# Another order for all engines' work in a block-sparse attention and spectral mixing kernel

## The chip, the core and the metric

The kernel runs on one core of a Trainium2 chip. The core has five instruction queues that matter here: TensorE (PE, matrix products and transposes; its weight loads are listed as PEld), VectorE (DVE), ScalarE (ACT), GpSimd (POOL) and SyncE (SP), which here does nothing but issue transfers. Each engine works through its own list in the order in which it was written and waits on semaphores for what the others have to finish. The metric is the device time of one execution in microseconds (us); less is better.

## The reference

Attention over 4 batches, 8 heads, 768 positions and 64 channels, then a mixing layer on its output (factors of the inputs left out):

```python
# attention: 16-wide local window, plus one summary key and value for each block of 32
k_sum = k.reshape(B, H, nb, 32, D).max(axis=3);  v_sum = v.reshape(B, H, nb, 32, D).mean(axis=3)
scores = concat(mask(scale * q @ k.T), scale * q @ k_sum.T + log(32))
a = softmax(scores);  x = a @ concat(v, v_sum)          # x: (4, 768, 512)
# mixing layer
theta = x @ w_theta
zr, zi = x * cos(theta), x * sin(theta)
u = x + einsum('ts,bsd->btd', w_tok_r, zr) + einsum('ts,bsd->btd', w_tok_i, zi)
out = u + relu(u @ w_ch)
```

All of it is float32. The kernel keeps that precision in the mixing layer by splitting each operand into a rounded high part and the remainder as low part, and adding three products (high by high, high by low, low by high). The weights arrive as 8-byte numbers and are turned into float32 on the chip.

## The kernel before

The function `attn_moe` first writes the whole program down as 2087 operations, each with the engines that may run it, what it reads and what it writes. Then `Program.issue` walks through a table, `ORDER`, which names the operations one after the other, each with the engine that gets it (P, A, V, G, S for PE, ACT, DVE, POOL, SP). That table alone sets the order on every engine and, where an operation may run on two engines, which of them it is. Buffers of a pool are handed out in the order in which they are first touched, so the table also sets who waits for which buffer.

The work, by the names used below. A batch has 6 tiles of 128 positions.

- **Weights** (`load_f64`): a raw block is loaded, then six or seven elementwise steps follow: magnitude (ACT or DVE), clip (DVE or POOL), a shift and two combining steps on DVE, the rounding to the high part (ACT or DVE, line 1342), the low part (DVE or POOL, line 1348). `wth0` to `wth3` hold w_theta, 12 blocks `wt` hold the two token matrices. At the end w_ch is loaded over `wth0` to `wth3`.
- **Attention tile** (`att_tile`, `att_half`, line 1476 onwards): scores `s` on PE, masked minimum on DVE (line 1489), exponential on ACT (line 1493), transpose `p` on PE, copy `pt`, product `av` on PE (line 1502), normalisation to `xn` (lines 1506 to 1515).
- **Turn and theta** (`turn_tile`, `theta_tile`): transpose of `xn` (line 1524), its high and low part `xh` and `xl`, 12 products with `wth` (line 1548), then a chain over ACT, POOL and DVE that reduces the angle and takes sine and cosine (lines 1556 to 1571), the products `w` and `zb` with `xn` (line 1579) and their high and low parts `zh`, `zl`.
- **Mixing** (`mix_step`, line 1600): for each batch two halves of the channels, for each half 6 tiles, for each tile 4 parts of 6 products (a part is one operation on PE). The sums stand in three banks `m`; the third is shared by the two channel groups. When a half is done, four additions on DVE (line 1616) take the sums out, and the result goes to `u_scratch` in memory.
- **Pool swap** (`swap_pools`): when all attention and theta work is done, its buffers are given up and those of the last stage take their place. No buffer of the last stage can be written before that.
- **Output units** (`out_unit`): 8 units; `u` is read back as four pieces `cu`, split into `cuh` and `cul`, multiplied with w_ch (line 1647, 16 operations of 3 products per unit), and added on DVE (line 1652).

PE interleaves all of these: attention and theta of one batch between the mixing parts of the batch before. The second half of the mixing of the last batch is left for after the pool swap and is interleaved with the first output units.

## Time and profile before

| | us |
|---|---|
| median of 3 runs | 501.67 |
| the runs | 500.26 to 502.81 |
| the profiled execution | 498.08 |
| its span, first to last instruction | 496.3 |
| PE busy | 453.7 |
| DVE, ACT, POOL busy | 319.1, 271.6, 102.6 |

A row of a group reads: line, engine, operation, output and inputs, size and count, then busy time, the mean of one in ns, and the idle time ahead of it with what ended it. In a timeline the first number is the start, the second the length, and square brackets hold the idle time before the instruction and what released it. SPq is SP issuing a transfer.

### The profile page before, as it was taken

What the parts mean: (1) busy time and instruction counts of PE and PEld (TensorE: products, weight loads), DVE (VectorE), ACT (ScalarE), POOL (GpSimd) and SP (SyncE); (2) the same over time, 40 slices, a digit from 0 to 9 for tenths busy, and PEclk for the clock granted to TensorE, in tenths of its full rate; (3) what the DMA queues carried; (4) which work ended last, traced back from release to release, by engine and by line L of the source; (5) the groups of instructions that cost most, each with busy time, mean ns of one, the idle gap of its engine ahead of it and who ended that gap; (6) DMA issues with size and microseconds to landing.
All of it is one profiled execution on the core that took longest, in us unless ns stands there. A gap on an engine that the chain in (4) does not pass through costs nothing.

```text
span 496.3 us, 10030 instructions
## 1 busy us (share of the span) xinstructions
PE 453.7 (91%) x3864; PEld 383.0 (77%) x3864; DVE 319.1 (64%) x909; ACT 271.6 (55%) x563; POOL 102.6 (21%) x124
## 2 busy tenths in 40 slices
PE   0876989999999999899979999999999499999997
PEld 0355767688887888788868888888878389999996
DVE  5999899977476687656764746435664494333454
ACT  2498999966455785746666775748753220101100
POOL 2033534324020120113011111220101430321021
PEclk9987999999999999999999999999999879999999
DMA  8999450444314640220413202210202600454653
GB/s 319 383 375 325 153 158 17 128 169 142 84 40 157 206 144 29 70 65 30 160 44 98 87 0 86 65 34 2 55 1 87 230 22 35 135 172 157 213 191 138
DMA packets 30767, 62.12 MB, mean 125 GB/s; under 512 B 3584, under 2 KB 14080, under 8 KB 30720
## 3 DMA queue, kind: packets, MB, share of 16 engines
q1 hardware_dynamic: 30720, 61.49, 37.2%
q8 instruction: 30, 0.49, 0.4%
q14 instruction: 17, 0.14, 0.1%
HBM read 48.90 MB, written 12.58 MB: 124 GB/s over the span
## 4 chain that ended last, share of the span: by engine, by line
PE 65%; DVE 13%; ACT 12%; DMA 4%; issue 3%; POOL 1%; SPq 1%; ACTq 0%; DVEq 0%
PE m L1600 29%; PE c L1647 14%; PE t L1548 10%; PE av L1502 4%; PE p L1496 3%; PE s L1476 3%; DVE e L1489 2%; ACT e L1493 2%; DMA vt<-cst 2%; PE av L1417 2%; DVE f L1391 1%; PE t L1524 1%; DMA q<-qg 1%; DMA cu<-u_scratch 1%; DVE xl L1529 1%
## 5 line engine op out<-in xcount | busy, mean ns | idle before, releaser
L1600 PE MATMUL m<-wt,zh 128*128 128x512 f32 (+1 forms) x768 | 171.9, 345 | 2.2 <-DVE x L1616 2.0
L1600 PEld LDWEIGHTS m<-wt,zh 128*128 128x128 f32 x768 | 119.8, 190 | 19.1 <-DVE x L1616 3.1
L1600 PE MATMUL m<-wt,zl 128*128 128x512 f32 (+1 forms) x384 | 99.1, 339 | 0.5 <-POOL zl L1348 0.4
L1493 ACT ACTIVATE e<-e,st 128x118 f32<-128x118 f32 x192 | 66.4, 388 | 28.0 <-DVE st L1489 27.8
L1647 PE MATMUL c<-cuh,wth 128*128 128x384 f32 x256 | 67.1, 343 | 7.0 <-DVE wth L1342 6.6
L1548 PE MATMUL t<-wth,xh 128*128 128x512 f32 x192 | 64.0, 416 | 5.9 <-ACT x L1342 2.8
L1600 PEld LDWEIGHTS m<-wt,zl 128*128 128x128 f32 x384 | 58.9, 189 | 9.9 <-POOL zl L1348 0.7
L1647 PEld LDWEIGHTS c<-cuh,wth 128*128 128x128 f32 x256 | 46.6, 191 | 8.2 <-issue 6.9
L1342 ACT CAST cuh<-cu 128x384 fp32r<-128x384 f32 x18 | 8.8, 510 | 78.3 <-DMA cu<-u_scratch 78.2
L1489 DVE CUSTOM_DVE_ANT_0 e<-s,cs 128x118 f32<-128x118 f32 x192 | 46.7, 272 | 7.0 <-PE p L1496 4.9
L1548 PEld LDWEIGHTS t<-wth,xh 128*128 128x128 f32 x192 | 35.0, 197 | 15.2 <-issue 5.0
L1647 PE MATMUL c<-cul,wth 128*128 128x384 f32 x128 | 43.9, 343 | 0.0
L1502 PEld LDWEIGHTS av<-v,pt 118*64 118x64 f32 x768 | 27.2, 138 | 15.4 <-issue 6.1
L1548 PE MATMUL t<-wth,xl 128*128 128x512 f32 x96 | 38.8, 404 | 0.0
L1652 DVE SCALAR_TENSOR_TENSOR cu<-c,cu 128x384 f32<-128x384 f32 x32 | 17.1, 553 | 30.9 <-PE c L1647 18.8
L1502 PE MATMUL av<-v,pt 118*64 118x65 f32 x768 | 33.5, 229 | 3.7 <-DVE xn L1515 1.6
L1348 POOL TENSOR_TENSOR cul<-cu,cuh 128x384 fp32r<-128x384 f32 x17 | 19.0, 1130 | 74.0 <-DVE cuh L1342 35.1
L1556 ACT ACTIVATE w<-t,bmagic 128x512 f32<-128x512 f32 x24 | 16.5, 686 | 30.5 <-PE t L1548 23.4
L1496 PE MATMUL p<-cs,e 128*118 128x128 f32 x192 | 30.6, 281 | 2.1 <-ACT pt L1342 2.1
L1348 POOL TENSOR_TENSOR zl<-w,zh 128x512 fp32r<-128x512 f32 x10 | 12.9, 1286 | 78.9 <-ACT zh L1342 60.9
L1558 POOL TENSOR_SCALAR w<-w 128x512 f32<-128x512 f32 x15 | 9.5, 632 | 87.9 <-ACT w L1556 87.8
L1348 POOL TENSOR_TENSOR zl<-zb,zh 128x512 fp32r<-128x512 f32 x15 | 20.1, 1345 | 36.2 <-DVE zh L1342 24.4
(85 smaller groups left out, 712.9 us busy)
## 6 DMA issues: line engine op xcount, KB each, us to landing
v<-vg SPq DMA_DIRECT2D x48, 195.0 KB, 2.8
q<-qg SPq DMA_DIRECT2D x24, 256.0 KB, 4.1
cu<-u_scratch SPq DMA_DIRECT2D x32, 192.0 KB, 3.3
out<-cu SPq DMA_DIRECT2D x32, 192.0 KB, 2.0
kn<-kT SPq DMA_DIRECT2D x6, 798.0 KB, 5.1
wt<-wtr SPq DMA_DIRECT2D x6, 768.0 KB, 9.1
wt<-wti SPq DMA_DIRECT2D x6, 768.0 KB, 10.2
f<-vT SPq DMA_DIRECT2D x12, 384.0 KB, 3.4
```

The costliest lines, as they stand in the source:

```text
L1348: op(f"VG tt {n}", lambda e: V[e].tensor_tensor(dst(), src(), hi().bitcast(F32), op=ALU.subtract), reads, writes)
L1417: product = lambda t, st: lambda: nc.tensor.matmul(pv.get()[:NB].rearrange("n p d -> n (p d)"), member(t), st(), start=(t == 0), stop=(t = ...
L1476: mm("s" if len(parts) == 1 else "s0", [lambda p=p, g=g, h=h, c=c, kk=kk: nc.tensor.matmul(sc[h].get()[ROW[g], p, c], q.get()[ROW[h], p, R ...
L1489: op("V ttr", lambda eng, n=n: nc.vector.tensor_tensor_reduce(e.get()[:, n], sc[n % 2].get()[:, 2 * a + n // 2], mask(m), -SCALE, 3.0e38, ...
L1493: op("A exp", lambda eng, n=n: nc.scalar.activation(e.get()[:, n], e.get()[:, n], AF.Exp, bias=st.get()[:, n:n + 1], scale=-1.0), [(st, n) ...
L1496: mm("tr", [lambda n=n: nc.tensor.transpose(tp.get()[:NK, n], e.get()[:, n], ident()) for n in range(NH)], [e, (cs, "ident")], [tp])
L1502: mm("av", [lambda n=n, g=g: nc.tensor.matmul(xa.get()[ROW[g], n], t.get()[:, n, ROW[g]], v[g].get()[:NK, NH * a + n], start=True, stop=Tr ...
L1548: calls = [lambda t=t, xx=xx, k=k, c=c: nc.tensor.matmul(th.get(), xx.get()[:, c], w_th[c].get()[:, k], start=(c == 0 and t == 0), stop=(c ...
L1556: op(f"A psumb {DM}", lambda e: nc.scalar.activation(r(), th.get(), AF.Identity, bias=bmagic.get(), scale=1.0 / TWO_PI), [th, bmagic], [R])
L1600: nc.tensor.matmul(acc[th], zz.get()[:, r, cc], w_t[s, r].get()[:, k, TT[th]], start=(s == r == t == 0 and (th == 0 or c == 0)), stop=(s = ...
L1647: calls = [lambda t=t, k=k, uu=uu, c=c, co=co, acc=acc: nc.tensor.matmul(acc.get(), w_ch[c].get()[:, k, co * P:(co + 1) * P], uu.get()[:, ...
L1652: op(f"V ttp {HT}", lambda e, co=co, acc=acc: nc.vector.scalar_tensor_tensor(u.get()[:, co], acc.get(), 0.0, u.get()[:, co], ALU.max, ALU. ...
```

## The change

The table `ORDER` is replaced. The operations, their sizes, the buffers and the pools stay as they are, and the numbers of operations on PE and POOL stay at 566 and 120; ACT has 471 in place of 467, DVE 713 in place of 717. All line numbers below the table fall by 29 (line 1342 becomes 1313, line 1616 becomes 1587). The table is a list of steps from one operation's number to the next; it has 1190 rows, now 1161, of which this is the head:

```diff
 ORDER = """
-V+4
-S+60
-V+1,+1,+1,+1
-S+12
...
+S+64
+A+1
+G+1
+V+1,-62,+63,+1,-66
...
```

Three places, as each engine's list reads before and now.

The first is DVE's list at the pool swap, which comes right after the last `zb`: `f` and `wth` belong to the conversion of w_ch, `cuh` and `cul` to an output unit, `x<-m` are the additions that empty the banks of the mixing. Before:

```order
L1579 TENSOR_TENSOR zb<-xn,w 128x512
L1386 TENSOR_SCALAR f<-f 128x512
L1342 CAST cuh<-cu 128x384
L1384 TENSOR_SCALAR f<-wth_4581 128x512
L1387 TENSOR_SCALAR f<-f 128x512
L1389 SCALAR_TENSOR_TENSOR f<-wth_4550,f 128x512
L1391 SCALAR_TENSOR_TENSOR f<-wth_4550,f 128x512
L1342 CAST wth_4622<-f 128x512
L1348 TENSOR_TENSOR cul<-cu,cuh 128x384
L1348 TENSOR_TENSOR wth_4622<-f,wth_4622 128x512
L1616 TENSOR_TENSOR x<-m_4251,x 128x256
```

Now:

```order
L1550 TENSOR_TENSOR zb<-xn,w 128x512
L1355 TENSOR_SCALAR f<-wth_4610 128x512
L1358 TENSOR_SCALAR f<-f 128x512
L1360 SCALAR_TENSOR_TENSOR f<-wth_4610,f 128x512
L1362 SCALAR_TENSOR_TENSOR f<-wth_4610,f 128x512
L1319 TENSOR_TENSOR wth_4622<-f,wth_4622 128x512
L1587 TENSOR_TENSOR x<-m_4323,x 128x512
L1587 TENSOR_TENSOR x<-m_4324,x 128x256 x2
L1587 TENSOR_TENSOR x<-m_4331,x 128x512
```

The rounding of a `cu` piece (second output unit) and the start of another block no longer stand inside the conversion of the first w_ch block; that conversion is now one run. Its magnitude moved from ACT to DVE, its clip from DVE to POOL, its rounding from DVE to ACT. On PE 14 mixing parts of the last batch now lie between its last theta product and the first output product; before there were 13.

The second is DVE's list where the first half of the mixing of the second batch ends (`x<-m`), among the work of later attention tiles. Before:

```order
L1579 TENSOR_TENSOR zb<-xn,w 128x512
L1489 ISA e,st<-s_2518,cs 128x118
L1489 ISA st 128x1
L1348 TENSOR_TENSOR zl<-zb,zh 128x512
L1616 TENSOR_TENSOR x<-m_2024,x 128x256
L1616 TENSOR_TENSOR x<-m_2031,x 128x512
L1489 ISA e,st<-s_2518,cs 128x118
L1489 ISA st 128x1
L1508 RECIPROCAL st<-st 128x4
L1616 TENSOR_TENSOR x<-m_2024,x 128x256
```

Now:

```order
L1313 COPY pt<-p 118x512
L1587 TENSOR_TENSOR x<-m_2025,x 128x512
L1587 TENSOR_TENSOR x<-m_2026,x 128x256
L1587 TENSOR_TENSOR x<-m_2033,x 128x512
L1587 TENSOR_TENSOR x<-m_2026,x 128x256
L1479 RECIPROCAL st<-st 128x4
```

The first of the four additions (`m_2023`) stood five rows above this piece. The four now stand together, behind the last mixing part of that half in the table; before, the first two came ahead of that part in the table, with other work between them.

The third is SP's list of loads near the start; `x<-vn` are the three loads for the block means of v, `cs` 128x128 is the identity that the transposes need. Before:

```order
L1339 DMA wth_113<-wth 128x1024
L1339 DMA cs<-cst 128x354
L1339 DMA x<-vn 128x2x512
L1339 DMA vt<-cst 128x44
L1339 DMA wt_124<-wtr 128x1536
L1339 DMA x<-vn 128x2x512
L1339 DMA q<-qg 128x512
L1339 DMA x<-vn 128x2x512
L1339 DMA v<-vg 96x520
```

Now:

```order
L1310 DMA wth_125<-wth 128x1024
L1310 DMA x<-vn 128x2x512 x2
L1310 DMA wt_181<-wtr 128x1536
L1310 DMA x<-vn 128x2x512
L1310 DMA q<-qg 128x512
L1310 DMA v<-vg 96x520
L1310 DMA cs<-cst 128x128
L1310 DMA v<-vg 96x520
```

The three loads stand a little earlier in the list, and the identity, which was the third load of all, is now the eighteenth.

More of the change, by code (lines that the diff above doesn't have):

```diff
@@ new lines @@
+A-253,+221,+1
+S+25,+1
+V-107,+111
+A-42,+47,-37
+G-219
+A+141
+P+155
+V-295,-6,+7
+P+177
+A+1,-184,+258,+1
+S+115
+A-228
+V+229
+P-149
+S-216,+379,+56
+V-178,-82
+G-184,+395,-1
+V-384
+P+292,-1,+3
+V-298
+P+207
+V-67
+P+157
+V-35
+A-83
+V-38
+A+79
+V+41
+A-53,+42,-108,+122
+V-1,-54
+P-29
+V+30
+A+177
+P-206
+A-180
+P+181
+G-177
+V+1
+A+260
+P-83,+71
+V-111
+P+78,+171
+A-170,+45,-83,+262,-1
+V-438,-5
+A+10
+P+287
+G-286
+V+210,-215
+A+257
+P+35
+A-45,-246
+V+176,+39,-38
+A+1
+P+38
+V-211,+1
+P+241,+12
@@ new lines @@
+V-42
+S+262
+V-43,-1,+2
+A+4,-223
+P+69,-27
+A+1
+V+1,+126
+P-102,+2,+101
+A+96
+P-84
+S-469,+6
+A+281
+V+1,+2
+A+41,+220,-93
+V+1,-170
+A+171
+V+56,+3
+P-162
+V+20,-86
+A+179
+V+48
+P-159,-27,+1,+1,+1,+26
+V+141
+A+5,+15
+V-5
+A+6
+P-52
+A+50
+S-28,-489,+596
+P-46
+A-48,+2
+P+2,-152
+A-22
+G+160,-159
+V+1,+40
+A+142
+V+37
+A-85
+V+1,+1,+82
+A+48
+V-93
+A-172,+222,-221
+G+263
+P-243,+3,+112,+37
+A+1
+V-172
+A+135
+P+48
+V+31,+15,-228
+A+1
+V+1
+P+18
+V+210,-95
+A+129
+P-242
+V+19
+P-17,+2,-3
+A+209,+31
@@ new lines @@
+V-91
+A+1
+V+10
+P+1
+V+32,+13
+A-12
+V-81,+91
+P+38
+A-32,-15,+2
+P+1
+V+47
+P-243
+V+197,-195,+2
+A+156,+130
+P-178
+V-106,+2
+P+105
+S+173,-281
+A+201
+S+29
+A-26
+P-95,+1
+A+1
+G+1
+V+44
+A+1,+129
+V-173
+P+92
+V+45
+P-243,+1
+V+4,+224,-219
+P-7,+148,-149,+4
+G+5
+P-3,+4
+V+4,+229,-228,+229
+S+216
+V+1
+A-230,-126,+1
+V+1
+S+218
+V-95
+A+17,+28
+V-255,+88
+P-103,+2
+S+447,-234
+V+8
+S-61
+P-156
+G+267
+P-266
+V+230,+213
+G-434
+V+88
+S+59,-173
+V+155,+1
+P+33
+V+1,+1,+1
+A+46,+1,+14
+P+31
+A-47,-35
@@ new lines @@
+P+2
+V-129,+1
+P+106
+G-195
+P+112,+7
+S+138
+V+7
+S+45
+A+5,-269
+G+1
+V+1,+1,+219
+S-501,+433
+P-109
+A+140,-12,+10,-32,+33,+39
+P-37
+V+50,-15
+A-173
+V-2,+189
+S-562
+P+396,+7
+S+80
+V-1
+G+2
+P+17
+V-127
+P+2
+V+138,+47
+P-163,-21,+1,+1,+21
+V+160
+P-158,+2
+A+148,+1,-15,-207
+V+1,+2,-1,+2
+A+231
+G+29
+P-190,+1,+2,-1
+A-27
+S-334
+A+519,-63
+G+92,-213
+V+1
+A+1
+V+164
+A+4
+P+3
+A+43
+V-94,+1
+A-120
+V+156,-155,+1,+1,+1
+P+127
+V+1,+1,+1
+P+80
+V-177
+A+143
+V+37
+S-64,+160
+A-270,+140,-12
@@ new lines @@
+A+34,-45,+1
+V-124,+79,+54
+A+4
+P-47
+V+1
+A+35
+P+1
+G-125
+A+47
+V+1,+85
+A+4
+V-88,+41
+A+36,+10
+P-230,-5,+2,+4,+1
+V+183,-41
+A+1,+87
+P-46,+35
+A+1
+V-33
+P+74
+A+52
+P-82
+V+34
+A-33
+V+30,+2,-79,+1,+90,+1
+A+35
+V-34
+A+32
+P-309,+3
+A+262,+2
+V+11,-16
+A+4
+P-79,+1,+1
+A+79
+P-78,-186
+V+216
+G+90
+A-30,-273
+G+1
+V+135,+1,+77,-76
+G+1
+P+86
+V+1
+S+73
+P+7,-44
+V-35
+A+47,-2
+S-24
+V+59
+P-309
+A+186
+G+1
+V+1
+A+77
+V-35
+P-226,-3,+5
+A+183,+88
+V-269
+A+182
+V-180
+S+293,-54
+P+17,-35
@@ new lines @@
+A+1
+P-28,+12,+6,-12,+1,-6
+V-6
+G+1
+V-191
+P+203,+1
+V+16
+A+6
+V-5
+S+7,-269,+40
+G+228,-3
+P-10
+V-9
+P+10,+1
+A+13
+P-32
+V+20
+S+1,-263
+P+253,-10
+S-197
+V+198
+P+10
+S-3
+P+4
+V+1
+S+1,-12
+G+30
+P+19,+1,+1,+1
+V+1
+S+1,+1
+P-24,+1,+1,+10,+1,+1
+S+19
+P-27,-3
+V+1
+S+26,-3
+V-2,+1
+S-21,-231
+P+233,+1,+1,+6
+V+1
+A+12
+V-18
+A+24
+P+8
+A-11
+S-14
+V+12
+S-18,+49
+P-24
+S+27
+A+1
+P-10,-6,-11,+6
+G-11,+3
+P+14,+1
+S+16,+3
+P-14,-11,+1
+V+1,+15
+P-5
+V+6
+P-5,-19,+1
+V+26,-25
+P+11
+V+7,-6
@@ L1236 @@
 P+3,+1
-V+1
-S+1
-P-16,+1,+1
 V+1
```

1914 lines of the change are left out of this document (770 added, 1144 removed).

## The prediction

> **What bounds the kernel now.** I read the page first: which engine is full, where it is not, and whether its clock holds.
>
> ```profile
> span 496.3 us, 10030 instructions
> ...
> PE   0876989999999999899979999999999499999997
> ...
> PEclk9987999999999999999999999999999879999999
> ...
> PE 65%; DVE 13%; ACT 12%; DMA 4%; issue 3%; POOL 1%; SPq 1%; ACTq 0%; DVEq 0%
> ```
>
> PE is full from about 100 us to the end but for one slice, the 32nd (384 to 397 us), and its clock dips there too. A change of order cannot shorten PE's own work; it can only take away PE's waits. So the next view is the waits of PE, longest in total first.
>
> ```profile
> PE s L1476 <- DVE ks L1411: 12.2, 3, 10.4
> PE c L1647 <- DVE wth L1342: 6.6, 1, 6.6
> PE t L1548 <- ACT x L1342: 2.8, 2, 1.6
> PE t L1548 <- DVE xl L1529: 2.3, 3, 1.5
> ...
> PE m L1600 <- DVE x L1616: 2.0, 3, 1.4
> ...
> PE av L1502 <- DMA v<-vg: 0.2, 1, 0.2
> ```
>
> The first is the start, when nothing is loaded yet. The second is one wait at the pool swap. PE's timeline shows it, and the chain of waits from there shows who caused it.
>
> ```profile
> 389.47 0.51 PE L1600 MATMUL m<-wt,zl 128*128 128x512 f32 x2
> 396.62 0.66 PE L1647 MATMUL c<-cuh,wth 128*128 128x384 f32 x1 [6.63 <-DVE wth L1342]
> 397.60 0.69 PE L1647 MATMUL c<-cuh,wth 128*128 128x384 f32 x1 [0.32 <-DVE wth L1348]
> ```
>
> ```profile
> 375.43 0.70 ACT w L1556
> ...
> 380.66 0.69 DVE zb L1579
> ...
> 385.64 5.67 DMA cu<-u_scratch
> ...
> 397.60 2.93 PE c L1647 x8
> 400.53 3.63 PE m L1600 x13
> ```
>
> The wait is not for the weights. In DVE's timeline the conversion of the first w_ch block began at 382.07, then DVE stood until 391.33 at a `cuh` rounding whose piece was still on its way, with the rest of the conversion behind it in the list:
>
> ```profile
> 382.07 0.43 DVE L1386 TENSOR_SCALAR f<-f 128x512 f32<-128x512 f32 x1 [0.73 <-ACT f L1382]
> 391.33 0.65 DVE L1342 CAST cuh<-cu 128x384 fp32r<-128x384 f32 x1 [8.84 <-DMA cu<-u_scratch]
> 391.90 0.41 DVE L1384 TENSOR_SCALAR f<-wth 128x512 int32<-128x512 int32 x1
> 392.69 0.98 DVE L1389 SCALAR_TENSOR_TENSOR f<-wth,f 128x512 int32<-128x512 int32 x1
> 393.70 1.37 DVE L1391 SCALAR_TENSOR_TENSOR f<-wth,f 128x512 uint32<-128x512 uint32 x1
> 396.86 0.68 DVE L1348 TENSOR_TENSOR wth<-f,wth 128x512 fp32r<-128x512 f32 x1
> ```
>
> **The change, part by part.** Sums are made against the profiled execution, span 496.3 and time 498.08; the runs shown have their median at 501.67, 3.6 us above it. I carry the difference in span over to the median.
>
> *The wait at the swap: 6.63 + 0.32 = 6.95 us.* The new order takes the `cuh` rounding out of the conversion. Does something else arrive late in its place? After the last theta product (375.4, where ACT's `w` starts) the angle chain runs to the end of `zb` at 380.66 + 0.69 = 381.35, so the buffers of the last stage come free 5.9 us after it; the new chain has the same steps, on other engines in part, and I leave it at 5.9. In that time and after it PE has mixing parts. A part is 6 products, and 48 products take 8.46 us in this stretch of the chain:
>
> ```profile
> 118.58 8.46 PE m L1600 x48
> ...
> 468.08 24.91 PE c L1647 x141
> ```
>
> So a part takes 1.06 us, and the 14 parts that now lie there 14.8 us. From the free buffers to the end of the parts there are 8.9 us. The conversion in that time, at this stretch's own slow prices: magnitude 0.41 (DVE), clip 0.72 (POOL), shift 0.41, combining 0.98 and 1.37 (DVE), rounding 0.61 (ACT), low part 0.68 (DVE): 5.2 us, and some 0.3 for six handovers. The `cu` piece runs beside it:
>
> ```profile
> 383.80 0.51 ACT L1342 CAST cuh<-cu 128x384 fp32r<-128x384 f32 x1 [1.76 <-DMA cu<-u_scratch]
> 392.41 0.72 POOL L1386 TENSOR_SCALAR f<-f 128x512 f32<-128x512 f32 x1 [0.64 <-DVE f L1384]
> 393.09 1.42 POOL L1348 TENSOR_TENSOR cul<-cu,cuh 128x384 fp32r<-128x384 f32 x1
> 394.48 1.70 POOL L1348 TENSOR_TENSOR zl<-zb,zh 128x512 fp32r<-128x512 f32 x1
> ```
>
> The first piece was there 2.5 us after the buffers came free; with rounding and low part that is 2.5 + 0.51 + 1.42 = 4.4. Both ways are ready 3 to 4 us before PE asks. I take the whole 6.95. Bounds: 0 kept of it at best; at worst a piece that takes the 5.67 of the chain and queues behind POOL's 1.70 is ready after 0.4 + 5.7 + 0.5 + 1.7 + 1.4 = 9.7, and 0.8 us stay.
>
> The combining step that took 1.37 at 393.70, beside a busy POOL, takes half as long where POOL stands:
>
> ```profile
> 19.82 0.69 DVE L1391 SCALAR_TENSOR_TENSOR f<-wth,f 128x512 uint32<-128x512 uint32 x1
> ```
>
> [...]
>
> *The clock after the wait: 2.9 us.* The windows behind it show TensorE at half clock:
>
> ```profile
> 393.00:395.00 2.00, 0.00 (x0) 0.00 (x0) 1.97 (x2) 0.22 (x1) 2.00 (x3) 0.50 0.06 22
> ...
> 401.00:403.00 2.00, 2.00 (x8) 1.71 (x8) 1.97 (x3) 0.00 (x0) 1.49 (x2) 0.50 0.00 0
> 403.00:406.00 3.00, 3.00 (x18) 2.60 (x18) 2.31 (x5) 0.62 (x1) 0.00 (x0) 0.96 0.02 5
> ```
>
> At 24.91 / 141 = 0.177 each, 8 output products take 1.41 us; they took 2.93. 13 mixing products at 0.176 take 2.29; they took 3.63. Together 2.86 us that go with the idle time. Bounds: 0, if a shorter wait still drops the clock, and 2.9. I take 2.9, since no wait is left. [...]
>
> *What the additions cost at the swap.* DVE now goes from the conversion straight to the four additions, which wait for the last mixing parts; the other w_ch blocks queue behind them. PE's list has 4 output operations (3 products, 0.53 us each) and 8 parts before it asks for the second w_ch block: 10.6 us. DVE has in that time the four additions (0.69, 0.42, 0.42, 0.69 in the rows further down) and eleven steps of 0.41 to 0.69, about 6.4 us: 8.6. No wait; I book 0.4 us of loss, bounds 0 and, with the eleven doubled as at 393.70, 4.4.
>
> *The end of a mixing half: 1 us.* In the second batch PE stood in the middle of a part:
>
> ```profile
> 208.52 0.74 PE L1600 MATMUL m<-wt,zh 128*128 128x256 f32 x3 [1.44 <-DVE x L1616]
> ```
>
> ```profile
> 205.64 0.69 DVE L1616 TENSOR_TENSOR x<-m,x 128x512 f32<-128x512 f32 x1
> 208.05 0.42 DVE L1616 TENSOR_TENSOR x<-m,x 128x256 f32<-128x256 f32 x1
> ```
>
> The product shares its bank with the sum that DVE was reading, and the reading was late behind `zb` and `zl`. With all four additions behind the last part this wait goes. The old order has such a crossing, an addition ahead of a last part, at three ends, and all waits of this kind are the 2.0 us of the list above; the new order has it at three other ends (first batch twice, third batch), with PE work of 0.6, 2.8 and 1.4 us between for an addition of 0.42 to 0.69. I take 1 us; bounds -3 and +2.
>
> *The middle otherwise: 1 us.* Two kinds of wait stand in the list above, theta for `x` and `xl`, 2.8 and 2.3. Counting PE work between a tile's turn and its first theta product for tiles 7 to 24: under 3 us at four tiles before, at one now. Between its last `av` and its turn: 2.2 us or less at nine tiles before, at one now. Steps on other engines are in part further back in exchange. Bounds -5 and +4.
>
> *The start: 1 us.*
>
> ```profile
> 10.00:20.00 10.00, 6.69 (x69) 2.84 (x70) 8.84 (x27) 3.63 (x7) 3.15 (x4) 1.00 1.04 395
> 90.00:100.00 10.00, 9.20 (x88) 6.81 (x87) 9.86 (x28) 9.16 (x19) 3.19 (x4) 1.00 0.41 127
> ```
>
> Loads run at 395 GB/s. Up to the third `x<-vn` 6723 KB were asked for, now 6403: 0.8 us earlier, and the identity 515 KB or 1.3 us after it, before the block means are done. From there to 100 us DVE and ACT are nine tenths full, with the same work. I take 1 us; bounds -4 and +4.
>
> Sum: 6.95 + 2.86 - 0.4 + 1 + 1 + 1 = 12.4 us, span 483.9, median **489.3 us**.
>
> **The rivals.** *The wait moves into the first output units* (second and third w_ch block late behind the additions). For: DVE's list there is long. Against: 2 us of cover. Doubled steps give a wait of 15.0 - 10.6 = 4.4, and with the clock's 2.9 the time is 501.7 - 12.4 + 7.3 = 496.6. *No change*: the swap gains its 9.4 and start and middle lose their lower bounds of 4 and 5; about 501. For: PE's middle has small waits at hundreds of places, and all of them are new. *Slower*: the `v` loads.
>
> ```profile
> v<-vg SPq DMA_DIRECT2D x48, 195.0 KB, 2.8
> ```
>
> They land in 2.8 us. SP's list is in order, with the waiting writes of `u_scratch` between them; PE work between the event that frees a `v` load and the product that needs it was 9.3 us or more from the second batch on, and is now 4.8 to 6.7 at four tiles. It decides once a late write in front holds them more than 2 us over that. At six ends of halves with 3.5 us each it costs 21, and the time is 501.7 - 12.4 + 21 = 510. Against: PE waited for `v` 0.2 us in all before.
>
> **Numbers.** The forecast 0.75, the moved wait 0.11, no change 0.07, slower 0.07. About 0.5% (2.5 us) is what a measurement of this kernel can tell from no change. The forecast's own range is 483 to 495; to leave out no more than 2 in 10 I go from 482 to 498. Faster 0.86 (both of the first), same 0.07, slower 0.07.
>
> **What would show it.** Right: no wait of PE over 2 us after 300 us, granted clock 1.00 through the swap, DVE's conversion of the first w_ch block in one piece of 4 to 6 us, PE's last product 10 to 14 us earlier. Wrong: PE `c` waiting for `wth` or `cuh`; `av` waiting for `v`; PE less busy than 9.2 us between 90 and 100 us.

## The result, and the profile after

The changed kernel takes 478.69 us (median of 4 runs, 478.44 to 480.48) beside 502.24 us of the kernel before (4 runs, 500.26 to 503.40): the ratio is 0.954, 95% interval 0.950 to 0.958. A second comparison with more runs gave 481.09 beside 500.36 us, ratio 0.959 (0.956 to 0.962). The forecast was 489.3 us with a range from 482 to 498: the direction is right, the gain, 23.6 and 19.3 us, was 1.9 and 1.6 times what was forecast, and the time lies below the range in both. The comparisons leave out a few slow executions: three of the kernel before at some 506 us, and four of others at 569 to 1502 us (in the one of 1104 us, profiled for swap_three, mixing products came 0.44 us apart in the mean, in place of 0.18 at full clock and 0.30 at half clock in middle_new, and its profile reads a clock of 1.00, so the half clock named in the expectation of swap_three_b is not shown).

The page of the changed kernel, the same rows as before:

```profile
span 476.6 us, 10041 instructions
...
PE   0875979999999999999999999999999999999997
...
PEclk9988899999999999999999999999999999999999
...
PE 78%; DVE 8%; DMA 6%; issue 3%; ACT 2%; POOL 1%; SPq 0%; ACTq 0%; POOLq 0%; DVEq 0%
```

The slice of the pool swap, where PE had stood, is full, and the clock reads 9 from the sixth slice to the end. The share of PE in the chain that ended last rose from 65 to 78%. The waits of PE, longest in total first:

```profile
PE s L1447 <- DMA q<-qg: 13.0, 1, 13.0
PE t L1519 <- DVE xl L1500: 6.6, 5, 4.2
PE av L1473 <- DVE xn L1486: 2.6, 2, 2.2
PE t L1495 <- DVE w L1530: 1.5, 2, 0.9
```

All four belong to the start: from 100 us to the end PE's waits of over 0.15 us add up to 0.6 us. There is no wait of an output product (`c`) and none of a mixing product (`m`). To see where the time went, the span is cut at three events that both kernels have: the end of theta 5 (attention of the first batch nearly done), the end of theta 23 (the last), and the end of the first output unit. Columns: length of the stretch, busy time and instructions of PE, PEld, DVE, ACT, POOL, the granted clock, then loads. Before:

```profile
0.00:103.50 103.50, 78.28 (x901) 56.86 (x902) 91.17 (x255) 82.01 (x165) 33.76 (x38) 0.95 0.67 233
103.50:375.30 271.80, 265.26 (x2359) 222.86 (x2359) 170.59 (x556) 173.46 (x367) 42.40 (x62) 1.00 0.25 78
375.30:420.80 45.50, 37.98 (x197) 33.46 (x196) 25.46 (x39) 9.83 (x18) 12.11 (x11) 0.89 0.28 96
420.80:496.30 75.50, 72.17 (x411) 69.83 (x410) 31.86 (x60) 6.34 (x13) 14.38 (x13) 0.99 0.50 166
```

and after:

```profile
0.00:101.70 101.70, 75.24 (x898) 56.23 (x899) 91.96 (x248) 80.86 (x162) 33.78 (x38) 0.95 0.65 221
101.70:366.10 264.40, 263.66 (x2357) 222.54 (x2356) 172.64 (x559) 176.65 (x389) 42.04 (x62) 1.00 0.27 84
366.10:402.80 36.70, 36.70 (x213) 33.12 (x212) 24.23 (x41) 9.08 (x16) 10.06 (x9) 1.00 0.37 123
402.80:476.60 73.80, 70.54 (x402) 68.86 (x400) 28.84 (x58) 7.11 (x15) 15.22 (x15) 1.00 0.52 174
```

Length less busy time is PE's idle time: 25.2, 6.5, 7.5 and 3.3 us before, 26.5, 0.7, 0.0 and 3.3 us after. The stretches do not hold quite the same PE instructions (the third has 16 more now), so below a stage's **loss** is used: its length less PE's own work in it, each operation at its price at full clock (theta product 0.695, mixing part 1.045, output operation 0.521 us, and so on); the last stage is taken up to PE's last product, 3.3 us before the end. In the two profiled executions:

| loss of PE, us | start, to theta 5 | middle, to theta 23 | swap, to end of unit 0 | last stage |
|---|---|---|---|---|
| before | 38.9 | 17.0 | 11.5 | 0.7 |
| after | 37.6 | 10.1 | 0.1 | 0.7 |
| gain | 1.3 | 6.9 | 11.4 | 0.0 |
| forecast | 1 | 1 + 1 | 6.95 + 2.86 - 0.4 = 9.4 | 0 |

They add up to 19.6 us, the difference of the two profiled executions (498.08 and 478.45). The sum of 12.4 us was short by 7.2 us: 4.9 in the middle, 2.0 at the swap, 0.3 in the start.

### The profile page after: what moved, and what is told of

It is laid out like the page before. It is cut to its first block, busy times and chain, and to the rows that moved or that the text cites. A ratio compares the mean times of both kernels' runs of the same rounds, so it can differ in the third digit from the quotient of the medians.

```text
span 476.6 us, 10041 instructions
## 1 busy us (share of the span) xinstructions
PE 446.1 (94%) x3864; PEld 380.7 (80%) x3864; DVE 317.7 (67%) x905; ACT 273.7 (57%) x582; POOL 101.1 (21%) x124
## 4 chain that ended last, share of the span: by engine, by line
PE 78%; DVE 8%; DMA 6%; issue 3%; ACT 2%; POOL 1%; SPq 0%; ACTq 0%; POOLq 0%; DVEq 0%
PE m L1571 38%; PE c L1618 14%; PE t L1519 12%; PE av L1473 5%; PE p L1467 4%; PE s L1447 3%; DMA wt<-wti 2%; PE t L1495 2%; DMA x<-vn 2%; DMA f<-vT 2%; DVE f L1360 1%; DVE f L1362 1%; DMA kn<-kT 1%; POOL wt L1319 1%; DVE e L1460 1%
## 5 line engine op out<-in xcount | busy, mean ns | idle before, releaser
L1519 PE MATMUL t<-wth,xh 128*128 128x512 f32 x192 | 62.8, 409 | 6.6 <-DVE xl L1500 6.6
L1618 PE MATMUL c<-cuh,wth 128*128 128x384 f32 x256 | 65.6, 337 | 0.0
L1519 PEld LDWEIGHTS t<-wth,xh 128*128 128x128 f32 x192 | 35.0, 194 | 15.1 <-DVE xl L1500 6.0
L1473 PEld LDWEIGHTS av<-v,pt 118*64 118x64 f32 x768 | 26.8, 138 | 14.6 <-issue 7.7
L1550 DVE TENSOR_TENSOR w<-xn,w 128x512 f32<-128x512 f32 x24 | 17.1, 712 | 18.5 <-ACT w L1542 18.5
L1319 POOL TENSOR_TENSOR cul<-cu,cuh 128x384 fp32r<-128x384 f32 x17 | 17.0, 1012 | 52.0 <-ACT cuh L1313 32.3
```

Of the source, the lines that this page charges most:

```text
L1319: op(f"VG tt {n}", lambda e: V[e].tensor_tensor(dst(), src(), hi().bitcast(F32), op=ALU.subtract), reads, writes)
L1473: mm("av", [lambda n=n, g=g: nc.tensor.matmul(xa.get()[ROW[g], n], t.get()[:, n, ROW[g]], v[g].get()[:NK, NH * a + n], start=True, stop=Tr ...
L1519: calls = [lambda t=t, xx=xx, k=k, c=c: nc.tensor.matmul(th.get(), xx.get()[:, c], w_th[c].get()[:, k], start=(c == 0 and t == 0), stop=(c ...
L1550: op(f"V tt {DM}", lambda e, z=z, hc=hc: nc.vector.tensor_tensor(z(), xn[b, i].get().rearrange("p h d -> p (h d)")[:, None, hc].broadcast_ ...
L1618: calls = [lambda t=t, k=k, uu=uu, c=c, co=co, acc=acc: nc.tensor.matmul(acc.get(), w_ch[c].get()[:, k, co * P:(co + 1) * P], uu.get()[:, ...
```

## The experiments

Three kinds of edit were run. `spliced` takes the table of one kernel up to a step and goes on with the other's, leaving out what has been issued already. `moved(table, ([ops], after), ...)` takes the named operations out of the old table and puts them behind the operation `after`, each on the engine it had. The third is a move in the new table. Where no other number stands, a time is the ratio to the kernel before on the same chip; the kernel before had medians of 500.4 to 501.2 us in these comparisons.

### The new order in one stage at a time

```diff
-        pr.issue(ORDER)
+        pr.issue(ORDER)                                            # before_again
+        pr.issue(spliced((LATER, 487), (ORDER, None)))              # start_new
+        pr.issue(spliced((ORDER, 487), (LATER, 1670), (ORDER, None)))  # middle_new
+        pr.issue(spliced((ORDER, 1674), (LATER, None)))             # swap_new
```

`LATER` is the new table. Expected of the kernel before, run again:

> The kernel before, unchanged, to see in a second profiled execution what its usual 502 us hold: the first profiled one took 498.1, while the others took 500.3 to 503.4. Theory 1 (the 4 us sit in the wait at the pool swap, which ends with a load): span about 500, PE's wait at the swap 9 to 11 us instead of 6.6, the start and the middle as before. Theory 2 (they sit in the start, while the loads come): last theta product of batch 0 about 4 us later than 103.5, the swap as before. Theory 3 (no one place): span near 496 again and the profile is merely a quick execution; then the same 4 us should show between span and time in no kernel.

Of the new order from shortly before the swap on:

> The old table up to its step 1674, just before the last tile's theta, then the new table for what is left. Main theory (the swap is worth its own 10 us, 6.95 wait, 2.9 clock, some of the rest): 10 us less in span, 488 to 492 in time, or 14 less if the unseen 4 us sit at the swap. Rival (the swap only gains because the new order's middle arrives there with other work done): less than 6 us.

Of the new order between:

> The old table up to step 487, the end of batch 0, then the new one up to step 1670, before the last tile's theta, then the old one. Main theory (the middle loses its single waits of 0.5 to 2.3 us and gets none new): 6 to 7 us less, about 495. My prediction's own size: 2 us less, about 500. Rival (the middle's gain is only time that the swap would have given back): 0.

Of the new order in the start alone:

> The new table up to its step 487, the end of batch 0, then the old one. Main theory: 1 to 2 us less, about 500.5. If the unseen 4 us sit in the start: 4 to 6 us less. Rival (the start is bound by the sum of DVE's and ACT's work, and the later products take back what was won): 0.

Measured, with the losses of the profiled executions:

| run | median us | ratio (95%) | start | middle | swap | last |
|---|---|---|---|---|---|---|
| before_again | 499.70 | 0.997 (0.994 to 1.000) | 39.3 | 17.0 | 10.6 | 1.7 |
| swap_new | 489.64 | 0.976 (0.971 to 0.982) | 42.0 | 17.1 | 0.1 | 0.8 |
| middle_new | 498.21 | 0.992 (0.989 to 0.995) | 41.3 | 9.6 | 11.0 | 7.1 |
| start_new | 505.88 | 1.010 (1.006 to 1.013) | 41.1 | 23.6 | 10.9 | 0.6 |

The swap alone is worth 11.9 us (0.0237 of 501), within the 488 to 492 us of the main theory. The new middle takes 7.4 us of loss away where it stands (17.0 to 9.6), but 6.4 come back in the last stage, behind the place where the tables are joined: PE waits there 2.4 us for `cul` and `cuh`, and the clock drops once more, to 0.50 (shown in the last section). The net is 3.8 us. The new start with the old continuation loses: right behind the cut the chain of waits goes through two loads for the summaries, 3.5 and 3.8 us, that DVE waits for. Both joins make waits of their own, so these two kernels do not price their stages. They suggest one thing: an order of one stage fits the order of the next, and a piece of it alone can be worth nothing or less.

One more thing is seen in the column of the start. before_again, swap_new and middle_new have the old start, like the kernel before, yet its loss is 38.9 and 39.3 in two of the four profiles and 41.3 and 42.0 in the others. In twelve of the fifteen profiled executions of the old start PE waits 1.1 to 2.2 us for `v` loads, which in the one profiled first cost 0.22 us; this row is from a kernel further down:

```profile
47.45 1.03 PE L1502 MATMUL av<-v,pt 118*64 118x65 f32 x16 [1.38 <-DMA v<-vg]
```

Over the fifteen the median loss is 41.0 us, so the execution that the forecast was built on was a quick one. The new start lost 37.6 and 37.0 in two profiles of the changed kernel, without a wait for `v`. But it scatters too: in start_new, which has the same steps up to there, the `av` product of tile 4 that begins at 78.4 us in the changed kernel begins at 81.3, and 2.4 of these 2.9 us are there at the first transpose already, with the first wait for `q` at 14.1 in place of 13.0 us. What the start is worth lies between 1 and 4 us and is not settled.

### The swap: taking away the blockers that the trace names

The forecast had read the wait of 6.63 us as the work of one `cuh` rounding inside the conversion of w_ch block 0. That is easily tried.

```diff
+        pr.issue(moved(ORDER, ([1836, 1792, 1804], 1718)))                                # dve_run
+        pr.issue(moved(ORDER, ([1799], 1767)))                                            # sp_first
+        pr.issue(moved(ORDER, ([1836, 1792, 1804], 1718), ([1799], 1767)))                # swap_both
+        pr.issue(moved(ORDER, ([1836, 1792, 1804], 1718), ([1799], 1767), ([1837, 1843, 1840], 1782)))  # swap_quiet
```

1836 is that rounding, 1792 the magnitude of block 3, 1804 a low part of unit 0; 1718 is the last of the four additions. 1799 is the load of piece 0 of unit 0, 1767 that of w_ch block 0. 1837, 1843 and 1840 are three low parts of unit 1 on POOL, 1782 the last step of block 1.

> The old table; on DVE alone the rounding of piece 0 of output unit 1 (it waited 8.84 us inside the conversion of the first w_ch block), the magnitude of w_ch block 3 and one low part stand behind the four additions of the last mixing half. Main theory (this one place in DVE's list is the swap wait): the conversion runs through by about 386 us and PE's wait for it, 6.63 us in the profile before, goes; what stays is piece 0 of the first output unit, which lands only at 390.2 and is rounded and split by 392.2, so PE still waits 1 to 3 us, and the low part that was moved back may cost another 1. Gain 4 to 8 us against the kernel before, about 495. Rival (SP's list is the blocker, since it issues piece 0 eighth): PE waits nearly as long, for cuh or cul now in place of wth, and the gain is under 2 us.

> The old table; SP asks for piece 0 of the first output unit right behind the first w_ch block, in place of eighth. Main theory (DVE's list is the blocker): DVE still stands at the rounding of unit 1's piece 0, which lands no earlier, so PE's wait for wth stays at 6 to 7 us; no change, within 1.5 us. Rival (SP's list is the blocker): a gain of 5 us or more.

> The old table with both of these moves, four operations in all. Main theory: with the run of DVE free and piece 0 early the whole wait goes and the clock after it, as with the new table from the swap on, which took 11.5 us off: gain 8 to 11 us, about 491, no wait of PE over 1.5 us between 385 and 400 us. Rival (the swap needs more of the new order than these four operations, the order of the other w_ch blocks and pieces too): half of it or less, 5 us at most, and a wait of 2 us or more that has moved into the first output units.

> The old table with the two moves of the swap, and POOL's three low parts of output unit 1 (3.6 us on POOL) back behind the conversion of block 1, so that POOL stands beside the conversions of DVE. If POOL beside DVE is what makes the second block late (steps of 1.2 to 1.8 us there, in place of 0.4 to 0.7), block 1 is ready 3 to 4 us earlier than the 28.1 us of the two moves, and 3 to 4 us are gained against the kernel before. If the order of the blocks decides: block 1 is ready at most 1.5 us earlier and the gain is under 2 us.

Measured: 0.999 (0.996 to 1.002), 0.999 (0.996 to 1.002), 0.999 (0.997 to 1.002) and 0.998 (0.995 to 1.000). None of the four gains anything that can be told. The main theory had sp_first right, and failed with dve_run (4 to 8 us) and swap_both (8 to 11); what swap_quiet can tell is said below. PE's timeline of dve_run, the rows with a wait, says why:

```profile
392.67 0.62 PE L1647 MATMUL c<-cuh,wth 128*128 128x384 f32 x2 [0.89 <-ACT cuh L1342]
393.76 0.44 PE L1647 MATMUL c<-cul,wth 128*128 128x384 f32 x1 [0.47 <-POOL cul L1348]
...
409.99 1.41 PE L1647 MATMUL c<-cuh,wth 128*128 128x384 f32 x2 [3.82 <-DVE wth L1342]
```

The wait of 6.63 is gone, as planned: 0.89 and 0.47 are left of it. But 17 us later PE stands again, now for block 1. It had been covered by the first wait. In the kernel before, the last step of block 1 ends at 411.2 + 0.69 = 411.9:

```profile
411.20 0.69 DVE L1348 TENSOR_TENSOR wth<-f,wth 128x512 fp32r<-128x512 f32 x1
```

Counted from the first step of the conversions (the magnitude of block 0 on ACT or DVE), the four blocks are done after

| run | block 0 | 1 | 2 | 3 | DVE idle until the last | loss at the swap |
|---|---|---|---|---|---|---|
| before | 16.2 | 30.5 | 29.5 | 25.2 | 10.8 | 11.5 |
| dve_run | 5.4 | 27.6 | 26.5 | 22.2 | 6.4 | 10.2 |
| swap_both | 4.3 | 28.1 | 27.0 | 22.7 | 8.0 | 10.0 |
| swap_quiet | 4.3 | 27.9 | 26.8 | 22.6 | 7.5 | 10.0 |
| after | 6.6 | 17.4 | 19.8 | 25.3 | 4.8 | 0.1 |

PE's old list has, behind the last mixing part of the first half (it ends 8.6 us after that first step), 4 output operations of 0.52 and 10 parts of 1.045 us before it asks for block 1, and then asks for blocks 2 and 3 within 2 us: with no wait that is at 21, 22 and 23 us (the expectations say 24 for the last). Block 1 comes 30.5 - 21.1 = 9.4 us later than that before, 6.5 in dve_run, 7.0 in swap_both, 6.8 in swap_quiet; the loss is each time 2 to 4 us more, for the lower clock behind the waits (0.50 before, in dve_run and in swap_both) and the short waits for `zh` and `zl`. The block that the trace names was only the first of four. Moving the waiting rounding left DVE with 6 to 8 us of idle time, most of it in another place, ahead of the additions, with blocks 1 to 3 behind them.

swap_quiet was to keep POOL still beside the conversions, and does not do it: a place behind 1782 in the table is no wait for 1782, and POOL's own list comes to these low parts at nearly the same time. POOL's rows from 397 us on, first in swap_both (where one more ran at 397.39), then in swap_quiet; each holds a low part of unit 0 besides:

```profile
400.81 3.60 POOL L1348 TENSOR_TENSOR cul<-cu,cuh 128x384 fp32r<-128x384 f32 x3
```

```profile
397.45 5.45 POOL L1348 TENSOR_TENSOR cul<-cu,cuh 128x384 fp32r<-128x384 f32 x4
```

In both, the last of them ends some 20 us after the first step, while block 1 is in work until 28. So the run says nothing on POOL beside DVE, though block 1 was ready at nearly the same time. Steps of DVE beside POOL take 1.2 to 1.8 us there in place of 0.4 to 0.7 (in swap_both the shift 1.23 and the `zl` 1.77, in place of 0.43 and 0.69). What speaks against this as the bound is swap_five below: DVE's steps are there 5.6 us in all over their shortest lengths, in dve_run 5.7, and yet the time falls.

### The swap: one order on all queues

```diff
+        pr.issue(moved(ORDER, ([1836, 1792, 1804], 1718), ([1799, 1775], 1767),
+            ([1776, 1777, 1778, 1779, 1780, 1781, 1782], 1774)))                          # swap_three
+        pr.issue(moved(ORDER, ([1836, 1792, 1804], 1718), ([1799, 1775, 1783], 1767), ([1808, 1805], 1802),
+            ([1776, 1784], 1774), ([1777, 1778, 1779, 1780, 1781, 1782], 1784), ([1809, 1806], 1782),
+            ([1845], 1842), ([1785, 1786, 1787, 1788, 1789, 1790], 1718), ([1807], 1798)))  # swap_four
+        pr.issue(moved(ORDER, ([1836, 1792, 1804], 1718), ([1799, 1775, 1802, 1783, 1808, 1805], 1767),
+            ([1688, 1728, 1800], 1768), ([1776, 1784], 1774), ([1803, 1809, 1806], 1784),
+            ([1777, 1778, 1779, 1780, 1781, 1782], 1784), ([1845], 1842), ([1785, 1786, 1787, 1788, 1789, 1790], 1718),
+            ([1729], 1718), ([1801], 1689), ([1810], 1735), ([1837, 1843, 1840], 1798), ([1807, 1846], 1798)))  # swap_five
```

1775 to 1782 are block 1 (its load first), 1783 to 1790 block 2; 1802, 1805 and 1808 load the other pieces of unit 0, 1803, 1806 and 1809 round them. PE's list is the old one in all three.

> The old table with the moves of the run before last (the rounding and two more steps of DVE behind the additions, piece 0 early on SP) and one more: w_ch block 1 is loaded right behind piece 0 and converted right behind block 0, ahead of block 3. Main theory (the swap is bound by the time until block 1 is converted, 30.5 us after the first step of the conversions before, 28.1 with the two moves, 16 to 17 with the new table, and PE without any wait asks for it some 22 us after that step): block 1 is ready by 15 us, PE's wait in the first output unit, 4.3 us with the two moves, goes down to 1 us or less, and the gain that was handed on is kept: 6 to 10 us less than the kernel before, about 493. Rival (the swap is bound by DVE's sum of work, or by POOL beside it, whatever block goes first): the wait moves on to block 2 or 3 and the gain stays under 3 us.

> The same kernel as the run with three moves, for a profile of an undisturbed execution, since the last one ran at half clock from end to end. The time of that run was the kernel before's. Theory (the last block decides): block 1 is ready before 15 us, and the last block still 27 us or later after the first step, because ACT's magnitude of block 1 or the steps of block 2 stand behind roundings whose pieces come late; PE waits 3 to 6 us for that block. Rival (the first block decides): PE waits over 4 us for block 0 or 1.

> The old table with the swap put in order by hand, PE's list untouched: SP loads block 0, piece 0, blocks 1 and 2, then the other pieces of the first unit; blocks 1 and 2 are converted right behind block 0 (1 ahead of the four additions, 2 behind them), block 3 after them, and the waiting cuh roundings stand behind. Theory (PE waits until the last of the four blocks is converted, 30.5 us after the first step of the conversions before, and it asks for the last one 24 us after that step; the block that the trace names is only the first of them. What makes the last one late is DVE's idle time in that stretch, 10.8 us before, 8.0 with two moves, 3.0 with the new table, at about 20 us of work in all three): the last block is ready by 22 to 25 us, no wait of PE over 1.5 us at the swap, 6 to 10 us less than the kernel before. Rival (PE's own list has to change too, since the old one asks for three blocks within 2 us; or POOL beside DVE stretches the work): the last block is ready at 27 us or later and the gain is under 3 us.

> The old table with the swap ordered by hand once more, PE's list untouched: what went wrong in the last hand order is mended (there SP's new order made ACT's first cuh rounding 6.8 us late, with the zh of the last mixing parts and the magnitude of block 1 behind it, and a zl stood behind block 2 on DVE: PE waited 9.8 us at these two). Now every queue has the same order: SP block 0, piece 0, block 1, piece 1, block 2, pieces 3 and 2; ACT zh first, then piece 0, the magnitudes, the other pieces; DVE block 0, block 1, the additions, zl, blocks 2 and 3; POOL zl and the low part of piece 0 first, those of unit 1 last. Theory (the last block's readiness sets the wait, and all queues have to carry one order): the last block is ready by 24 us after the first step where it was 28 to 30.5, PE's waits at the swap sum to 2 us or less, and the time is 6 to 10 us below the kernel before. Rival (PE's own list or DVE's work beside POOL is the bound): last block at 26 us or later, 3 us or less gained.

| run | median us | ratio (95%) | blocks 0, 1, 2, 3 done after | DVE idle | loss at the swap |
|---|---|---|---|---|---|
| swap_three | 500.60 | 0.998 (0.995 to 1.001) | 4.3, 15.1, 30.4, 27.0 (of swap_three_b) | 9.4 | 9.8 |
| swap_four | 503.42 | 1.008 (1.004 to 1.011) | 4.3, 14.6, 20.3, 30.2 | 9.2 | 14.3 |
| swap_five | 493.40 | 0.985 (0.979 to 0.991) | 6.2, 9.3, 15.2, 22.6 | 2.6 | 2.7 |

With block 1 early (swap_three), block 2 was the last, at 30.4 us. That is what swap_three_b expected of the block. Its wait of 3 to 6 us for it did not come (0.2 us): PE was held up ahead of it, 3.10 us for a `zh` and twice over 1 us for an addition and a `zl`. With block 2 early too (swap_four) it got worse. The reason is in ACT's timeline and in PE's:

```profile
389.99 0.51 ACT L1342 CAST cuh<-cu 128x384 fp32r<-128x384 f32 x1 [6.82 <-DMA cu<-u_scratch]
390.41 0.61 ACT L1342 CAST zh<-w 128x512 fp32r<-128x512 f32 x1
```

```profile
391.07 1.65 PE L1600 MATMUL m<-wt,zh 128*128 128x512 f32 x4 [5.23 <-ACT zh L1342]
...
407.28 1.00 PE L1600 MATMUL m<-wt,zl 128*128 128x512 f32 x2 [4.55 <-DVE zl L1348]
```

SP loaded the two w_ch blocks ahead of piece 1, but ACT's list still rounded piece 1 first: it stood 6.82 us for that load, and behind it stood the `zh` that the last mixing parts need. On DVE a `zl` stood behind block 2 in the same way. In swap_five the lists of SP, ACT, DVE and POOL have the same order, and nothing that is needed soon stands behind something that comes late. PE's only waits of some length there:

```profile
395.50 1.07 PE L1600 MATMUL m<-wt,zh 128*128 128x512 f32 x4 [1.01 <-DVE x L1616]
...
409.09 0.45 PE L1647 MATMUL c<-cul,wth 128*128 128x384 f32 x1 [0.72 <-DVE cul L1348]
```

Blocks 1, 2 and 3 are ready after 9.3, 15.2 and 22.6 us, all ahead of 21, 22 and 23, and 7.6 us are gained (0.0151 of 501) where swap_new gained 11.9. So one consistent order on SP, ACT, DVE and POOL is the cause of about two thirds of the swap's gain, and PE's own list is not needed for that. That it acts through the readiness of the later blocks is read from these times and not tried by itself: swap_five also brings `zh`, `zl` and the pieces of `cu` forward. The rest, some 4 us, was not taken apart; PE's new list is a candidate, since it spreads its requests: in the changed kernel it asks for blocks 1, 2 and 3 at 18.8, 23.5 and 25.6 us, and they are ready at 17.4, 19.8 and 25.3.

### The middle: two waits at a time

```diff
+        pr.issue(moved(ORDER, ([1063], 1062), ([888], 885)))     # mid_two
+        pr.issue(moved(ORDER, ([888], 885), ([936], 1155)))      # mid_three
```

888 is the addition that PE waited 1.44 us for in the second batch, 885 the last part that shares its bank. 1063 is a `zl` of tile 13 on POOL, which stood behind a copy that had waited 11.4 us. 936 is an addition of the second half, for which DVE stood 2.56 us at 254.8, with the copies of `x` of tile 15 (up to 1155, its `xl`) behind it. The kernel before, DVE and then PE:

```profile
254.76 0.42 DVE L1616 TENSOR_TENSOR x<-m,x 128x256 f32<-128x256 f32 x1 [2.56 <-PE m L1600]
```

```profile
257.85 0.69 PE L1548 MATMUL t<-wth,xh 128*128 128x512 f32 x2 [1.52 <-DVE xl L1529]
```

> The old table with two moves in the middle: on POOL the low part zl of tile 13 goes ahead of the copy of the k load that held POOL for 11.4 us (behind it ACT's next w and the theta chain stood, and PE waited 1.0 and 1.5 us at tile 15); on DVE the addition that reads the bank before the last mixing part of the second batch goes behind that part (1.44 us). Main theory (the middle's gain of some 8 us is a handful of such single places): gain 3 to 5 us. Rival (the places are taken up by slack later, or the gain is spread over hundreds of small waits): 0 to 1.5 us.

> The old table with two additions on DVE moved in the middle: the one that reads the bank before the last part of the second batch's half goes behind that part (1.44 us of PE's wait), and the one that stood 2.56 us for a mixing part at tile 15, ahead of the copies of x from the sum, goes behind these (PE waited 1.52 us for xl). Main theory (in the middle a wait of PE that DVE's list makes is taken away by a move on DVE): both waits go and the offset of PE's time over its work at the end of tile 15, 10.8 us over that at tile 5 in the profile before, is 2.5 to 3.5 us lower; the median 1 to 3 us lower. Rival (as at the swap, what is freed there is waited for at the next step): under 1 us, and the median the same.

mid_two measured 1.000 (0.996 to 1.003), as its rival had it, mid_three 0.992 (0.989 to 0.995), 4.1 us less. The bank wait is gone in both. In mid_two one wait at tile 15 only changed its name, and the other stayed; these are PE's waits of 0.9 us or more from 200 to 262 us:

```profile
247.83 0.62 PE L1476 MATMUL s<-k,q 64*64 64x118 f32 x12 [0.99 <-POOL k L1342]
...
257.94 0.70 PE L1548 MATMUL t<-wth,xh 128*128 128x512 f32 x2 [1.53 <-DVE xl L1529]
```

The copy of `k` that was passed over is now the one that PE waits for. In mid_three, with 936 behind the `xl`, one wait is left there, which the kernel before had too:

```profile
252.41 0.65 PE L1496 MATMUL p<-cs,e 128*118 128x128 f32 x4 [1.04 <-ACT pt L1342]
```

The loss of the middle falls from 17.0 to 14.8 (mid_two) and 13.2 (mid_three). So two additions on DVE that stood ahead of their time account for 3.8 of the 6.9 us that the new middle gains. mid_two's 2.2 us should just show in its time and do not; that stays unexplained.

### Both places together

```diff
+        pr.issue(moved(ORDER, ([888], 885), ([936], 1155), <the moves of swap_four>))     # hand_all
+        pr.issue(moved(ORDER, ([888], 885), ([936], 1155), <the moves of swap_five>))     # hand_five
```

> The old table with this order of the swap and the two additions of DVE moved in the middle, which alone gave 0.9918 (3 to 4 us less). If both are causes of the gain of the new table, each at its place, they add: 9 to 14 us less than the kernel before, 487 to 491, with 6 to 10 us left to the changed kernel (its start and the small waits of the middle). If the time is taken back downstream, less than the larger of the two alone.

> The same, with the two additions of DVE moved in the middle, which alone gave a ratio of 0.9918. If both places are causes and nothing is taken back downstream, the gains add: 3 to 4 us below the kernel with the swap alone, 9 to 14 us below the kernel before.

hand_all: 500.38 us, 0.999 (0.996 to 1.002). Beside swap_four (1.008) that is 0.9 of a hundredth less, the middle's gain; its expectation of 9 to 14 us failed with swap_four's order. hand_five: 489.95 us, 0.979 (0.973 to 0.984), 10.8 us less, 3.2 below swap_five. The product of the two alone would be 0.992 x 0.985 = 0.977. Within the intervals the gains add; little is taken back downstream.

### The start, and the changed kernel again

> The changed kernel as it is, for the spread of its executions. Theory A (the quick profile before: what the profiled spans leave unexplained, some 4 us, lies in the start, where executions of the old table differ by the landing of v and q loads and those of the new one do not): the executions lie within 2.5 us of each other, where those of the kernel before spread over 6 to 8 us, its profile has no wait for v over 0.5 us in the first 100 us, and the ratio is again 0.953 to 0.958. Theory B (the first comparison had slow executions of the kernel before by chance): the ratio is 0.960 or more.

> The changed kernel with three operations moved in its start: ACT's two copies of x of tile 1 ahead of the angle step of theta 0, in which ACT loads a table for 1.3 us, and DVE's xl of that tile ahead of steps of the token weights. PE waits 4.2 us there for xl, its longest wait after the first. If the start is bound by this one list: the wait falls by 2 to 3.5 us and the time by as much (0.994 of the changed kernel's). If it is bound by the sum of DVE's and ACT's work, which are nine tenths full: the wait is passed on to theta 2 or the first mixing parts, and the time is that of the changed kernel, within 1 us.

```diff
-        pr.issue(ORDER)
+        pr.issue(moved(ORDER, ([238, 236], 195), ([237], 236)))  # after_x1, on the new table
```

The changed kernel again: 481.09 us (6 runs, 478.29 to 482.68), ratio 0.959 (0.956 to 0.962). Neither expectation holds whole: its executions spread over 4.4 us and not 2.5, and the ratio is just under 0.960. There is no wait for `v` in its start. The medians differ by 19.3 us here, no more than the spans of the first pair do; the 3.9 us that the first comparison showed beyond the spans did not come again.

after_x1 moves the copy of x of tile 1 (238), its rounding `xh` (236) and its `xl` (237) ahead of work that PE does not wait for. It took 481.62 us, ratio 0.963 (0.958 to 0.968): no faster than the changed kernel. PE's waits in its start:

```profile
45.66 0.73 PE L1519 MATMUL t<-wth,xh 128*128 128x512 f32 x2 [1.27 <-DVE xl L1500]
53.53 1.13 PE L1473 MATMUL av<-v,pt 118*64 118x65 f32 x16 [4.80 <-ACT pt L1313]
```

The wait for `xl` fell from 4.18 to 1.27 us, and 8 us later PE stood 4.80 us for a `pt`. ACT's timeline shows what is in front of that `pt`: two table loads and, between them, what had been put off.

```profile
44.90 1.28 ACT L1541 ACT_TABLE_LOAD   x1
...
48.42 1.28 ACT L1464 ACT_TABLE_LOAD   x1
```

The rival of that run was right: in the start, where DVE and ACT are nine tenths full (54.2 and 52.0 of the 55 us from 45 to 100 in the changed kernel), the wait that was taken away was passed on.

## Why the prediction was right and wrong

**The step that failed** is the price of the middle. Its two terms, 1 us for the end of a mixing half and 1 us for the rest, stand against 6.9 us of loss that went. Both were cut down because the new order has crossings and short distances of its own in other places, and that exchange did not happen: between theta 5 and theta 23 PE's waits add up to 5.8 us in the kernel before (2.0 for additions, 1.8 for `xl`, 1.0 for a `pt`, 1.0 in three others) and to 0.6 us in the changed one.

**The bound.** Right: PE's own work stayed, its waits went. From 100 us on PE waits 0.6 us in all.

**The wait at the swap, 6.95, the clock behind it, 2.86, the additions, -0.4.** Near in size: 9.4 us were forecast, 11.4 us of loss went (11.9 in time by the splice alone). The conversion of block 0 is one run of 6.6 us, where 5.2 and 0.3 had been worked out, and PE goes from the last mixing part straight to the first output product:

```profile
380.20 0.51 PE L1571 MATMUL m<-wt,zl 128*128 128x512 f32 x2
380.55 0.51 PE L1618 MATMUL c<-cuh,wth 128*128 128x384 f32 x2
```

The 2.0 us of cover for the second block are 18.8 - 17.4 = 1.4. But the reason given, "The new order takes the `cuh` rounding out of the conversion", is not the cause: done alone it gains nothing. The price of 6.95 was near by luck, because the first wait covered most of what the later blocks would have cost. The 2.86 us hang on the execution too: behind the same wait the clock was at half for 10.24 us (393.01 to 403.25) in the one that the forecast was built on, and for some 7 us in before_again, by its mean clock of 0.92 from 376 to 421 us. What failed as an explanation is that the question "Does something else arrive late in its place?" was put to the new table only; put to the old one it would have shown block 1 ready at 411.9, long behind what PE could have reached.

**The end of a mixing half, 1 us.** Wrong in size. Two additions out of their place on DVE cost 3.8 us of loss (mid_three). The wait at 208.52 was seen and its 1.44 us cut to 1, since the new table has three such crossings elsewhere; those cost nothing, there is no wait for `m` left. The second one was not seen: PE's wait stood under `xl`, 1.52 us, while DVE had waited 2.56 us for a mixing part with the copies of `x` behind it. It was a wait of the same kind, found by following the late engine's list and not PE's releaser.

**The middle otherwise, 1 us.** Wrong in size: some 3 us (6.9 - 3.8). The counts of cover per tile, "under 3 us at four tiles before, at one now", pointed the right way and were priced far too low. Of the small waits in this part nothing was tried one by one.

**The start, 1 us.** 1.3 in the pair, so right by the sum; against the median of the old start it would be 3.7, and by start_new's profile of the new one less, so the size stays open. That "PE waited for `v` 0.2 us in all before" was true of the one execution only.

**"I carry the difference in span over to the median."** The pair of profiled executions differs by 19.6 us, the medians by 23.6 and 19.3. The step holds within the scatter of a few runs; in the first comparison the medians differ by more than the spans, which makes 3.4 us of the miss of 10.6 (the forecast counts from 501.67, the median it was given); the short terms make 7.2.

**The rivals.** None came true in the changed kernel. *The wait moves into the first output units* is what dve_run (3.82 us at 409.99), swap_both and swap_quiet did, each a hand-made half of the change. *Slower* through late `v` loads did not come; the loads were late in the old order. With the upper bounds of the last three terms, 2, 4 and 4, the sum would have been 19.4 and the time 482.3: the range ended where all bounds were met at once, and the middle alone passed its two (6.9 against 2 + 4).

Of the signs named, four came (no wait over 2 us after 300 us, clock 1.00 through the swap, PE 9.7 of 10 us busy between 90 and 100 us, no wait of `av` for `v`); the conversion took 6.6 in place of 4 to 6 us, and PE's last product came 19.6 us earlier in place of 10 to 14.

**What stays open.** The last 4 us at the swap beyond swap_five, the 3 us of the middle that are not two additions, what the start is worth, whether POOL beside DVE costs time at the swap, why mid_two's gain does not show in its time, and why executions of the changed kernel lie between 478 and 483 us. No version beat the changed kernel.

## What to carry to other kernels

The releaser that a trace names for a long wait is the first late thing, not the only one: before pricing its removal, write down when each later input is ready and when the waiting engine would ask for it with no wait, and take the largest difference. Queues that run in order must carry one common order: in swap_four SP had a new order where ACT's list still had the old one, ACT stood 6.8 us with urgent work behind it, and the gain came only when SP, ACT, DVE and POOL agreed. A place in the table binds only the engine whose list it is in: to hold POOL back, something that POOL waits for has to be moved. And profile the kernel before more than once: one quick execution hid some 2 us of its usual loss.
